# Linear attention and an ELU feed-forward on one core: the instruction orders of blocks three to six, solved anew

## The chip, the core and the metric

The kernel runs on one core of a Trainium2 chip. The metric is the device time of one execution in microseconds (us); the median of three runs of the kernel before is 292.15 us (291.99 to 292.51). The core has five engines with instruction streams of their own: TensorE (PE in the profile; its weight loads are listed apart as PEld), VectorE (DVE), ScalarE (ACT), GpSimd (POOL) and SyncE (SP), which here only issues transfers. Each engine executes its stream in order; an instruction that needs another engine's result waits at a semaphore, and everything behind it in the same stream waits with it.

## The reference

```python
# q, k, v: [8 batches, 8 heads, 576 positions, 64]
q_s = exp(q - max) / sum over the 64 features
k_s = exp(k - max) / sum over the 576 positions
kv  = einsum('bhsd,bhse->bhde', k_s, v)
attn = einsum('bhsd,bhde->bhse', q_s, kv)
x = attn.transpose(0, 2, 1, 3).reshape(4608, 512)
h = x @ w_in                                   # [4608, 2048]
g = where(h > 0, h, exp(min(h, 0)) - 1)        # ELU
out = g @ w_out                                # [4608, 512], float32
```

## The kernel before

**Attention.** Work goes by units, `n` = 0 to 15, each with half of a batch entry's eight heads. For a unit, k, v and q tiles are loaded (`load`, L361: 128 partitions by 1152 floats, 576 KB). ScalarE takes the exponential of k in place (L401) and of q (L397); VectorE sums q's exponentials over the features (L423) and inverts the sums (L425); POOL or VectorE scales q by them into `QS` (L435); v is converted to bfloat16 in `VB` by ScalarE or POOL (L279 with output VB). `QS` is transposed, from unit 4 on by a transposing transfer on the SP queue (L472) into `QT`, which ScalarE or POOL widens to `qsT` (L279). TensorE multiplies k and v (L509, 72 small matmuls a unit in the paired form), VectorE scales the result into the block-diagonal `MBLK` (L518, L522), and TensorE multiplies it with `qsT` (L540). The result is copied from PSUM into `XT`, the input of the feed-forward (L279 with output XT), by ScalarE or VectorE. There is one buffer for the v tiles of most units (`VR0`, called `vR0` in the planner), so the next v load cannot start before the conversion of the tile before has read it.

**Feed-forward.** Its rows go in nine blocks of 512 (`j` = 0 to 8). In each, eight groups (`g`) of two hidden tiles are computed on TensorE with eight 512-column matmuls (`hg_mm`, L622) into one of two pairs of PSUM banks. For each group ScalarE takes the exponential from PSUM into `GE` (L672) and then `relu(1 - exp)` in place (L674), and VectorE combines both with the PSUM value into `GR` in two halves (L678). Only then can TensorE overwrite that pair of banks with the next but one group.

**Output.** Blocks 0 and 1 are multiplied with `w_out` directly (L699, 512 columns). From block 2 on, pairs of rows are multiplied by a Strassen-like scheme with seven products in place of eight (`pair`, L832, 256 columns). It needs sums and differences of the `GR` tiles (`add_sum`, L783, by VectorE or POOL; some go to the tile `SB`) and, once, combinations of `w_out` (`combos`, L759, into `TB`). VectorE adds the products from PSUM into `OSB` (L841), PSUM copies to `OSB` are made by ScalarE or VectorE (L279), and SP stores `OSB` (L728).

**What sets the order.** Every instruction, or short run of matmuls, is an operation with a number, given in the order in which `program` creates it (0 to 1401). Its dependencies follow from the tiles that it reads and writes. The strings in `ORDER` list, for each engine, the numbers in the order in which it executes them. Where an operation may run on either of two engines, it runs on the one in whose list it stands:

```python
if alts:
    eng = self.home.get(len(self.ops))
    eng = eng if eng in alts else next(iter(alts))
    dur = alts[eng]
```

So a number that goes from the list "act" to the list "gp" moves that operation from ScalarE to POOL. Semaphore waits are placed from the dependencies. The lists are written out; nothing is reordered when the kernel is built, and the planner's own durations only decide how many spare matmuls fill TensorE's start.

Operations that the text below names:

| Numbers | What they are |
|---|---|
| 219 | k load; 234 is ScalarE's exponential of it |
| 362, 370 | VectorE's L678 of a group; TensorE's group that overwrites its banks |
| 396 | `w_out` combination into `TB`, 1024 columns, read by matmuls 506 |
| 403, 404 | narrower combinations, 512 columns |
| 451, 466, 467 and 474 | sums on `GR` tiles (256 columns; 474 has 512) |
| 473 | sum into `SB`, 512 columns; 461: L832 matmuls that 467 waits for |
| 601, 604, 767 | conversions of v tiles that share the buffer `VR0` |
| 602, 605 | the v loads into `VR0` after 601 and after 604 |
| 640, 643, 693, 695, 707, 779, 791 | sums on `GR` tiles; 779 is read by matmuls 787 |
| 666, 678, 699, 708, 729, 741 | groups of L622, eight matmuls each |
| 671, 672 | VectorE's L841 addition; the L832 matmuls that follow in its bank |
| 683 to 685 | L832 matmuls; sum 695 waits for 684 |
| 700 to 703 | L672, L674 and the two L678 of group 699, whose banks group 729 overwrites |

Of the kernel before, what the change touches and what calls it, by code (L numbers as in the profile page):

```python
# [50 lines left out]
    "act": (  # L51
# [12 lines left out]
    "dve": (  # L64
# [37 lines left out]
}  # L102

# [1013 lines left out]
```

## Time and profile before

| | |
|---|---|
| Time, median of 3 runs | 292.15 us |
| Time of the profiled execution | 292.0 us |
| Its span, first to last instruction | 290.2 us |
| Granted TensorE clock, mean | 0.999 |
| Busy: PE, PEld | 280.1, 243.7 us |
| Busy: DVE, ACT, POOL | 231.5, 212.1, 160.3 us |
| HBM read, written | 36.70 MB, 9.44 MB |

The profiled execution takes 1.8 us more than its span. The changed part of the orders begins at 62.1 us on SP, 67.4 us on VectorE, 69.2 us on TensorE, 71.4 us on POOL and 73.2 us on ScalarE, and ends at 203.6, 213.6, 214.0, 216.1 and 208.3 us.

A row of a view by groups gives line, engine, operation, output and input tiles, shape and count, then busy time in us and the mean of one in ns, then the idle time of the engine just before these instructions, with what ended it ("<-"). A row of the timeline gives start and length in us and merges neighbours of one kind. In the view of transfers, the time to landing runs from the issue to the arrival of the last byte. Busy times of matmuls overlap, since TensorE pipelines them and their ends are modelled.

### The profile page before, as it was taken

The page shows a single profiled execution, that of the slowest core. Times are in us where ns is not written, and L with a number is a line of the kernel's source. Part 1 is how long each engine was busy: PE and PEld are TensorE (multiplying, and loading weights), DVE is VectorE, ACT ScalarE, POOL GpSimd, SP SyncE. Part 2 cuts the span into 40 slices and gives each one's busy share as a digit, 9 for nine tenths or more (in the row PEclk, how much of TensorE's full clock was granted, in tenths as well). Part 3 has the DMA queues.
Part 4 walks back from the last instruction along what each step waited for, and adds up shares of the span by engine and source line. Part 5 has one row for each costly group of instructions (what it writes and reads, how often), then busy time and mean ns, then how long its engine had stood idle before and what let it go on. Part 6 is the DMA issues. An engine that isn't in the chain of part 4 may idle for free.

```text
span 290.2 us, 5483 instructions
## 1 busy us (share of the span) xinstructions
PE 280.1 (97%) x2176; PEld 243.7 (84%) x2176; DVE 231.5 (80%) x432; ACT 212.1 (73%) x237; POOL 160.3 (55%) x159
## 2 busy tenths in 40 slices
PE   2899999999999999999999999999999999999995
PEld 0488887888888899989899998989999999989995
DVE  3758847886699998898998879797785978668884
ACT  4858838989999877989887788857687546655510
POOL 1992443426356679409776793845417712794441
PEclk9999999999999999999999999999999999999999
DMA  7999999897989724775686457322211001400244
GB/s 260 395 369 388 390 388 357 219 212 253 267 246 292 209 103 111 248 189 172 133 267 198 122 82 277 69 48 52 63 36 38 0 2 30 114 0 20 56 97 123
DMA packets 36474, 50.04 MB, mean 172 GB/s; under 512 B 16352, under 2 KB 18144, under 8 KB 36448
## 3 DMA queue, kind: packets, MB, share of 16 engines
q1 hardware_dynamic: 29680, 33.96, 42.6%
q0 software_dynamic: 6528, 15.47, 17.6%
q8 instruction: 17, 0.28, 0.4%
q10 hardware_dynamic: 240, 0.26, 0.3%
q14 instruction: 9, 0.07, 0.1%
HBM read 36.70 MB, written 9.44 MB: 159 GB/s over the span
## 4 chain that ended last, share of the span: by engine, by line
PE 91%; DVE 3%; DMA 2%; POOL 2%; ACT 0%; SPq 0%; issue 0%
PE PS L622 44%; PE PS L832 32%; PE PS L699 9%; PE PS L540 3%; DMA KR<-in_k_dram 2%; PE PS L509 2%; DVE GR L678 1%; POOL W L379 1%; DVE QS L435 0%; DVE ZQ L423 0%; POOL VB L279 0%; PE PS L459 0%; POOL QS L435 0%; DVE MBLK L522 0%; ACT GE L674 0%; SPq L361 0%
## 5 line engine op out<-in xcount | busy, mean ns | idle before, releaser
L622 PE MATMUL PS<-XT,W 128*128 128x512 f32 x576 | 141.5, 393 | 0.1
L622 PEld LDWEIGHTS PS<-XT,W 128*128 128x128 f32 x576 | 105.3, 188 | 21.1 <-DVE GR L678 0.3
L678 DVE SCALAR_TENSOR_TENSOR GR<-PS,GE 128x512 fp32r<-128x512 f32 x112 | 76.7, 686 | 20.6 <-ACT GE L674 19.2
L672 ACT ACTIVATE GE<-PS 128x1024 f32<-128x1024 f32 x56 | 57.4, 1024 | 43.1 <-PE PS L622 36.2
L783 POOL TENSOR_TENSOR GR<-GR 128x256 fp32r<-128x256 f32 (+1 forms) x50 | 48.5, 981 | 47.7 <-DVE SB L783 29.0
L674 ACT ACTIVATE GE<-GE 128x1024 f32<-128x1024 f32 x56 | 59.4, 1060 | 1.5
L832 PE MATMUL PS<-TB,GR 128*128 128x256 f32 x336 | 52.5, 283 | 0.0
L832 PE MATMUL PS<-W,GR 128*128 128x256 f32 x336 | 52.2, 283 | 0.0
L832 PEld LDWEIGHTS PS<-TB,GR 128*128 128x128 f32 x336 | 46.5, 191 | 1.4 <-DVE OSB L841 0.3
L832 PEld LDWEIGHTS PS<-W,GR 128*128 128x128 f32 x336 | 46.5, 191 | 1.1
L435 POOL TENSOR_TENSOR QS<-QR,RZQ 128x1152 f16<-128x1152 f32 (+1 forms) x15 | 27.7, 1845 | 29.5 <-DVE RZQ L425 26.2
L841 DVE TENSOR_TENSOR OSB<-OSB,PS 128x256 f32<-128x256 f32 x84 | 34.8, 416 | 10.8 <-PE PS L832 9.3
L699 PE MATMUL PS<-W,GR 128*128 128x512 f32 x128 | 32.2, 394 | 0.0
L783 POOL TENSOR_TENSOR GR<-SB,GR 128x256 fp32r<-128x256 f32 (+1 forms) x26 | 25.4, 985 | 8.2 <-PE PS L832 7.4
L699 PEld LDWEIGHTS PS<-W,GR 128*128 128x128 f32 x128 | 23.6, 188 | 4.5
L423 DVE TENSOR_REDUCE ZQ<-QR 128x18 f32<-128x1152 f32 (+2 forms) x18 | 21.7, 1208 | 5.8 <-ACT QR L421 4.9
L783 POOL TENSOR_TENSOR SB<-GR 128x256 fp32r<-128x256 f32 (+1 forms) x19 | 18.6, 981 | 11.8 <-PE PS L832 7.1
L401 ACT ACTIVATE KR<-KR 128x1152 bf16<-128x1152 f32 x16 | 18.4, 1158 | 2.7 <-DMA KR<-in_k_dram 2.7
L783 DVE TENSOR_TENSOR GR<-GR 128x256 fp32r<-128x256 f32 (+1 forms) x34 | 19.9, 595 | 0.1
L397 ACT ACTIVATE QR<-QR 128x1152 f32<-128x1152 f32 x14 | 16.2, 1158 | 1.8 <-DMA QR<-in_q_dram 1.7
L279 POOL CAST VB<-VR 128x1152 bf16<-128x1152 f32 (+1 forms) x11 | 12.2, 1111 | 8.6 <-DMA VR<-in_v_dram 8.6
L832 PE MATMUL PS<-W,SB 128*128 128x256 f32 x104 | 16.8, 283 | 0.0
(67 smaller groups left out, 265.1 us busy)
## 6 DMA issues: line engine op xcount, KB each, us to landing
out_dram<-OSB SPq DMA_DIRECT2D x61, 128.0 KB, 2.4
QR<-in_q_dram SPq DMA_DIRECT2D x12, 576.0 KB, 5.4
KR<-in_k_dram SPq DMA_DIRECT2D x12, 576.0 KB, 5.4
VR<-in_v_dram SPq DMA_DIRECT2D x12, 576.0 KB, 5.7
W<-in_moe_w_out_dram POOLq DMA_DIRECT2D x4, 1024.0 KB, 16.3
QR<-in_q_dram POOLq DMA_DIRECT2D x4, 576.0 KB, 11.9
VR<-in_v_dram POOLq DMA_DIRECT2D x4, 576.0 KB, 13.0
KR<-in_k_dram POOLq DMA_DIRECT2D x4, 576.0 KB, 14.0
```

The costliest lines, as they stand in the source:

```text
L397: S.add("act", t_act(1152, False), lambda e: e.activation(flat(q), flat(q), AF.Exp), key - 3, X=[f"qR{i}0", f"qR{i}1"])
L401: S.add("act", t_act(1152, False), lambda e: e.activation(ek[:, :, :, :].rearrange("p h c d -> p (h c d)"), flat(k), AF.Exp), key - 2, X=[ ...
L423: S.add("dve", t_dve(m), lambda e, qp=qp, zp=zp: e.tensor_reduce(zp, qp, AX.X, ALU.add), key - 3, R=[f"qR{i}{x}" for x in xs], W=[f"ZQ{i}{ ...
L435: lambda e, qp=q[:, :, a:b, :], rz=rz, dst=qs[:, :, a:b, :]: e.tensor_tensor(dst, qp, rz, ALU.mult),
L622: last = e.matmul(P[:, t * 512:(t + 1) * 512], self.W1[:, kc, tt * 128:(tt + 1) * 128], self.XT[:, kc, rc:rc + BLK], start=(kc == 0), stop ...
L672: S.add("act", t_act(1024, True), lambda e: e.activation(ge, P, AF.Exp), key, W=own, X=banks)
L674: S.add("act", t_act(1024, False), lambda e: e.activation(ge, ge, AF.Relu, bias=1.0, scale=-1.0), key, X=own)
L678: S.add("dve", t_dve(512 if j else 1024), lambda e, u=u: e.scalar_tensor_tensor(*(x[:, :, u, :] if j else x for x in (gt, P)), 0.0, ge[:, ...
L699: last = e.matmul(dst, self.tile(jb, jj, ts), self.W2[:, jj, c0:c1], start=(jj == 0), stop=(jj == 15))
L783: lambda e: e.tensor_tensor(dst, a, b, op), key, R=R, W=W, X=X, after=after)
L832: last = e.matmul(dst, a[i][:, y_, :], b[i][:, y_, :], start=start and i == 0 and y_ == 0, stop=stop and i == len(grps) - 1 and y_ == z - ...
L841: S.add("dve", t_dve(256), lambda e: e.tensor_tensor(dst, a, b, ALU.add), key, R=R, W=W, X=X, after=after)
```

## The change

The lists of all five engines are replaced in the stretch from the third block to the sixth, about operations 288 to 1041. The operations, their numbers and their dependencies stay. 73 operations stand in another engine's list:

| From | To | Operations |
|---|---|---|
| DVE | POOL | 24: 14 sums of 256 and 5 of 512 columns, 4 `w_out` combinations, one scaling of q |
| POOL | DVE | 19: 11 sums of 256 and 8 of 512 columns |
| DVE | ACT | 14: 8 copies to `OSB`, 6 copies to `XT` |
| ACT | POOL | 8: 3 conversions of v, 5 widenings of `qsT` |
| ACT | DVE | 6: 5 copies to `XT`, one copy to `OSB` |
| POOL | ACT | 2 conversions of v |

ScalarE's list has 241 entries instead of 239, VectorE's 419 instead of 432, POOL's 166 instead of 155; TensorE's 457 and SP's 119 are in another order. The core of the diff (the rows that hold the places named above):

```diff
     "pe": (
-        "651 625 626 627 634 652 653 645 662 663 656 657 664 658 666 672 683 673 684 674 685 587 "
-        "678 687 688 589 689 714 690 691 715 692 716 699 598 708 725 719 726 720 721 727 606 729 "
-        "781 735 782 736 737 741 783 785 786 787 788 789 814 790 815 797 816 819 808 820 825 826 "
+        "625 651 626 652 653 627 634 645 656 657 658 662 663 664 683 684 685 666 672 673 674 587 "
+        "678 589 687 688 689 714 715 690 691 692 716 598 699 708 719 725 720 726 721 727 606 729 "
+        "735 781 782 736 737 741 783 785 786 787 788 797 789 790 814 815 816 808 825 819 820 826 "
...
     "act": (
-        "543 544 433 437 564 565 441 576 577 586 746 635 636 646 647 601 667 668 588 603 679 680 "
-        "600 597 700 713 701 709 757 710 730 731 752 742 743 767 798 799 809 769 810 830 831 909 "
+        "543 544 591 433 564 565 621 576 577 586 650 635 636 646 647 746 603 667 668 679 686 680 "
+        "600 604 700 701 709 710 607 757 730 731 784 742 743 909 813 798 799 809 810 830 831 770 "
...
     "gp": (
-        "163 132 164 201 206 204 209 228 231 307 238 397 401 325 393 417 406 398 462 473 450 435 "
-        "451 466 465 467 396 477 428 474 527 478 531 476 583 438 641 639 632 633 629 631 640 643 "
-        "594 644 693 695 749 694 696 604 706 705 707 791 779 793 780 795 792 796 805 760 802 803 "
+        "163 132 164 201 206 204 209 228 231 307 393 238 397 310 318 401 325 394 406 417 398 328 "
+        "400 473 451 403 466 404 467 474 396 477 435 428 529 531 532 528 530 431 438 539 583 630 "
+        "616 629 639 641 633 594 642 695 640 643 693 601 644 597 704 749 706 705 767 791 707 779 "
...
     "sp": (
-        "8 9 10 11 12 13 205 207 210 220 229 219 180 230 236 309 308 190 183 356 184 347 239 181 "
-        "249 357 189 319 187 248 326 186 348 320 418 392 377 391 329 378 338 419 494 495 511 510 "
-        "429 430 436 339 557 584 558 585 574 573 449 439 660 661 448 595 602 677 676 596 750 605 "
+        "8 9 10 11 12 13 205 207 210 220 229 187 189 183 181 219 180 190 230 184 236 309 308 357 "
+        "186 239 356 347 249 319 326 348 248 378 320 391 418 392 377 338 329 419 494 495 339 429 "
+        "510 511 436 430 558 557 584 585 573 574 439 448 449 595 661 660 602 677 676 596 605 751 "
```

81 rows, old and new, of the table ORDER are left out of this document.

## The prediction

> **What bounds the kernel now.** I read the page first (busy shares, then the chain of work that ended last), then busy time by stretch over the part whose orders change, then the waits of the weight loads, then single stretches of the timeline. The first two rows are of the page, the next four of the view by stretch (start and end, length, busy time and instructions of PE, PEld, DVE, ACT, POOL; granted clock, DMA share, GB/s), the last two all waits of the weight loads from 60 us to the end.
>
> ```profile
> PE 280.1 (97%) x2176; PEld 243.7 (84%) x2176; DVE 231.5 (80%) x432; ACT 212.1 (73%) x237; POOL 160.3 (55%) x159
> PE 91%; DVE 3%; DMA 2%; POOL 2%; ACT 0%; SPq 0%; issue 0%
> ...
> 67.00:100.00 33.00, 32.90 (x291) 27.46 (x290) 27.84 (x45) 31.38 (x35) 17.78 (x13) 1.00 0.85 248
> 100.00:140.00 40.00, 40.00 (x319) 36.07 (x318) 36.08 (x76) 34.64 (x38) 27.27 (x25) 1.00 0.55 159
> 140.00:180.00 40.00, 40.00 (x321) 36.12 (x320) 34.42 (x65) 32.89 (x35) 26.84 (x26) 1.00 0.72 194
> 180.00:216.00 36.00, 36.00 (x292) 32.48 (x291) 30.41 (x63) 25.56 (x30) 18.58 (x17) 1.00 0.24 56
> ...
> PEld PS L832 <- DVE OSB L841: 0.3, 1, 0.3
> PEld PS L622 <- DVE GR L678: 0.3, 1, 0.3
> ```
>
> TensorE is busy without a break at clock 1.00 all through the part that changes, and 91% of the chain is TensorE's. A busy TensorE need not be at its peak, so I count its work. The rows below: two pieces of the chain with nothing but one kind of matmul (start, length), the matmuls between 69.17 and 213.97 us (the first and the last place at which TensorE's order differs), and three neighbouring pieces of its timeline.
>
> ```profile
> 218.37 3.68 PE PS L622 x16
> 222.05 4.79 PE PS L832 x40
> ...
> L622 PE MATMUL PS<-XT,W 128*128 128x512 f32 x312 | 78.0, 394 | 0.1
> L832 PE MATMUL PS<-W,GR 128*128 128x256 f32 x192 | 30.6, 282 | 0.0
> L832 PE MATMUL PS<-TB,GR 128*128 128x256 f32 x184 | 29.1, 283 | 0.0
> L699 PE MATMUL PS<-W,GR 128*128 128x512 f32 x45 | 11.2, 390 | 0.0
> L832 PE MATMUL PS<-W,SB 128*128 128x256 f32 x64 | 10.1, 282 | 0.0
> ...
> 153.72 0.36 PE L540 MATMUL PS<-qsT,MBLK 128*128 128x192 f32 x2
> 154.02 0.78 PE L509 MATMUL PS<-VB,KR 64*64 64x65 bf16 x72
> 154.72 2.12 PE L622 MATMUL PS<-XT,W 128*128 128x512 f32 x8
> ```
>
> A 512-column matmul takes 3.68/16 = 0.23 us, a 256-column one 4.79/40 = 0.12 us. So 357 x 0.23 = 82.1 us and 440 x 0.12 = 52.8 us, together 134.9 of 144.8 us. A group of 72 small L509 matmuls takes 154.72 - 154.02 = 0.70 us, and there are five in the stretch (3.5 us); the 41 of L540 take about 0.15 us each by the pair at 153.72 (6.2 us). That makes 144.6 us. What can be won between the first and the last changed matmul is a few tenths: the two named waits, 0.6 us in all, and no more than about that again in what the rounding hides.
>
> **The change part by part.** Nothing is added or removed: the same 1402 operations with the same dependencies. Seventy-three change engine; the rest of the diff is order. TensorE's count of matmuls of each kind between its first and last difference is the same, so its own work is worth nothing either way, and only a wait can cost it time. The moves, each at the time of a row of the same shape:
>
> ```profile
> 140.57 0.74 POOL L783 TENSOR_TENSOR GR<-GR 128x256 fp32r<-128x256 f32 x1
> 157.40 1.30 POOL L783 TENSOR_TENSOR GR<-SB,GR 128x512 fp32r<-128x512 f32 x1 [1.70 <-PE PS L832]
> 151.91 1.15 POOL L279 CAST VB<-VR 128x1152 bf16<-128x1152 f32 x1
> 106.18 2.41 POOL L759 TENSOR_TENSOR TB<-W,TB 128x1024 fp32r<-128x1024 f32 x1
> 138.90 1.15 ACT L279 ACTIVATE VB<-VR 128x1152 bf16<-128x1152 f32 x1
> ```
>
> POOL receives 24 operations from VectorE (14 narrow sums at 0.74, five wide sums and three narrow combinations at 1.30, a wide combination at 2.41 and one 1152-column q scaling, taken at the same 2.41: 25.6 us) and eight 1152-column conversions from ScalarE (9.2 us); it gives 19 sums to VectorE (11 x 0.74 + 8 x 1.30 = 18.5 us) and two conversions to ScalarE (2.3 us). Net POOL works 14.0 us more in the stretch, ScalarE and VectorE less (14 PSUM copies also go from VectorE to ScalarE, six back). In the four rows above, POOL worked 90 of 149 us, so it has room on the average; VectorE, with 129 of 149 and 36.1 of 40 between 100 and 140 us, is relieved. On the average this speaks for the new orders, but TensorE did not wait for VectorE before, beyond the 0.6 us.
>
> The matmuls of operations 683, 684 and 685 (8 x 0.12 = 0.96 us) now stand ahead of group 666, so that operation 672, which waited 0.3 us for VectorE's L841 addition, comes later; I count -0.3 us. The other wait, before operation 370 at 86.6 us, keeps its neighbours and stays.
>
> Seven of the eight stores of the first block's output now stand earlier on SP, four of them ahead of k load 219:
>
> ```profile
> 62.08 1.31 SPq L361 DMA_DIRECT2D KR<-in_k_dram  x1
> 70.67 1.17 ACT L401 ACTIVATE KR<-KR 128x1152 bf16<-128x1152 f32 x1
> 72.15 1.03 ACT L672 ACTIVATE GE<-PS 128x1024 f32<-128x1024 f32 x1 [0.32 <-PE PS L622]
> ```
>
> At about 0.6 us of the queue each (two take 1.12 at 154.13, below) load 219 leaves at about 64.5 instead of 62.08 and lands 5.4 us later, at 69.9; ScalarE reads it at 70.67 and was then idle for 0.32 us. Cover of 0.8 us, so I count 0; with a landing of 6.5 us it would be 71.0, late by 0.3, which the idle time takes up. SP's other moves put a store (0.6 us) ahead of a load or behind one; 0 as well, and the three places below hold the loads for which that is not so.
>
> The tightest new place is at 138 to 154 us. Conversion 604 of a v tile moves from POOL to ScalarE, where it stands directly ahead of exponential 700; conversion 601, which frees the v buffer for the load 602 that 604 waits for, moves from ScalarE to POOL and stands behind four sums. So ScalarE now stops in the middle of its L672/L674 work until a load lands, and behind it wait 700, 701, then VectorE's 702 and 703, then TensorE's group 729, which overwrites their PSUM. The chain starts when matmuls 684 end:
>
> ```profile
> 149.84 1.03 ACT L672 ACTIVATE GE<-PS 128x1024 f32<-128x1024 f32 x1 [0.70 <-PE PS L622]
> 151.02 1.06 ACT L674 ACTIVATE GE<-GE 128x1024 f32<-128x1024 f32 x1
> 152.15 1.40 DVE L678 SCALAR_TENSOR_TENSOR GR<-PS,GE 128x512 fp32r<-128x512 f32 x2
> ...
> L361 SPq DMA_DIRECT2D VR<-in_v_dram x1: 580/580/580, 142.4 to 142.4; - x1
> DMA to landing us min/median/max: 6.4/6.4/6.4
> ...
> L361 SPq DMA_DIRECT2D VR<-in_v_dram x1: 383/383/383, 153.1 to 153.1; - x1
> DMA to landing us min/median/max: 4.0/4.0/4.0
> ...
> DMA to landing us min/median/max: 4.0/5.4/6.5
> ...
> 140.39 0.60 SPq L361 DMA_DIRECT2D KR<-in_k_dram  x1
> 141.03 1.32 SPq L472 DMA_TRANSPOSE QT<-QS  x1
> 154.13 1.12 SPq L728 DMA_DIRECT2D out_dram<-OSB  x2
> 155.29 0.59 SPq L361 DMA_DIRECT2D QR<-in_q_dram  x1
> ```
>
> POOL: sums 695, 640, 643, 693 and conversion 601, 0.74 + 1.30 + 0.74 + 1.30 + 1.15 = 5.2 us; then the load; then 604 (1.15), 700 (1.03), 701 (1.06), 702 and 703 (1.40): 4.6 us. With about 0.3 us of hand-overs that is 10.1 us and the load. TensorE's work from the end of 684 to 729 is 32 matmuls of 512 columns, 50 of 256, three pairs of L540 and one pair with 72 of L509: 7.4 + 6.0 + 0.9 + 1.0 = 15.3 us. The load may therefore take 5.2 us. The same load took 6.4 us before, right behind a k load and a transpose; all 27 loads on this queue from 60 to 180 us lie between 4.0 and 6.5. In the new order the k load and the transpose are long done, and two stores and a q load follow it: just the company of the load at 153.1 us, which took 4.0. So the stall is between 0 (1.2 us in hand) and 6.5 - 5.2 = 1.3 us; I take a load of 5.0 to 5.4 us, as it is nearer to the 4.0 row by its company but its followers come sooner, and count 0.2 us, the upper end.
>
> The second tight place follows from it: the next v load, 605, is issued when 604 has read the buffer; POOL's 767 (1.15) waits for it and behind it stand sums 791, 707 and 779 (1.30 + 0.74 + 0.74), the last of which matmuls 787 need. From 604's end that is the load and 4.1 us; TensorE has 3.6 us to 729 and 16 x 0.23 + 22 x 0.12 = 6.3 us from there to 787, so 5.8 us for the load. At the median of 5.4 it holds; I count 0.
>
> The third is POOL between 98 and 109 us: sum 473 and seven more operations up to combination 396 (three narrow sums at 0.74, two combinations and a wide sum at 1.30, then 2.41), 9.8 us in a row. Sum 467 waits for matmuls 461; from there POOL has 0.74 + 1.30 + 2.41 = 4.5 us, and TensorE 16 x 0.23 + 16 x 0.12 = 5.6 us until matmuls 506, which read 396. About 1 us in hand; I count 0.
>
> ```profile
> L783 DVE TENSOR_TENSOR SB<-GR x11: 413/682/1451, 90.9 to 192.2; 128x256 fp32r<-128x256 f32 x7, 128x512 fp32r<-128x512 f32 x4
> 149.34 2.63 POOL L783 TENSOR_TENSOR GR<-GR 128x512 fp32r<-128x512 f32 x2
> ```
>
> These rows show what can eat that: VectorE's wide sum takes 0.68 us alone and once 1.45 us, with POOL's two sums beside it at 2.63 instead of 1.30 + 0.74 = 2.04 us. The Trainium skill, page "SBUF — State Buffer", section "Who interferes with whom", has a rule for it: a VectorE instruction with two SBUF inputs and a GpSimd instruction that reads SBUF exclude each other, and the later one stands still until the other ends. The trace agrees with it here.
>
> Sum: 292.0 us (the profiled execution; its span is 290.2, with 1.8 us around it) - 0.3 + 0.2 = 291.9; the median of the runs, 292.15, lies 0.15 above the profiled one, so 292.1.
>
> **The rivals.** First, slower: ScalarE stands still for v load 602. If loads 602 and 605 take 6.4 us as the one at 142.4 us did, TensorE loses 6.4 - 5.2 = 1.2 us at 729 and 6.4 - 5.8 = 0.6 us at 787, 1.8 in all: 292.1 - 0.2 + 1.8 = 293.7. It decides from a load of 5.2 us. For it: the exponential at 149.84 us waited for TensorE, and now a DMA stands in the same line. Against: the company of the load. Second, also slower: POOL as the bound from 98 to 109 us. Each meeting of two-input operations can cost up to 1.45 - 0.68 = 0.77 us; five VectorE sums lie in that stretch, two full meetings (1.54) use up the 1 us in hand and 0.5 more: 292.6, and with the sums behind late too up to 293.2; I take 292.9. Against: three of the five come before sum 467's wait for 461, which evens them out. Third, faster: both named waits go and nothing is late: 292.15 - 0.6 = 291.5. Against: the neighbours of 370 stay. Fourth, that the orders leave no more slack than before: TensorE then stays the bound with about as many close hand-overs, and the time is the forecast's; this is part of it.
>
> **How the numbers follow.** Forecast (292.1, alone 291.6 to 292.7) 0.57; late v loads 0.27 (293.7); POOL 0.11 (292.9); faster 0.05. The range goes from 291.6, below which I leave 4 in 100, to 294.0, above which both stalls and followers of them would lie: it is the first rival's 293.7 and a little. A difference of 0.2% (0.58 us) is about what a measurement of this kernel can tell from none. Faster by more than that is only the third rival: 0.04. Slower are the first rival, half of the second, and a tail of the forecast: 0.37. The rest, 0.59, within.
>
> **What would show it.** Right: TensorE busy 40.00 of 40.00 in the stretches from 100 to 180 us again; the wait of L832's weight loads for L841 gone; POOL's busy time up by some 14 us, VectorE's down; a wait of ScalarE's VB conversion for the v load of about 1 to 2 us, without an entry for L622 behind VectorE's L678 near 153 us. Wrong: weight loads of L622 waiting for L678 there by 1 us, or of L832 for POOL's or VectorE's sums near 110 or 160 us; waits of over 0.6 us in sum anywhere; or a stretch of TensorE that is shorter than 144 us.

## The result and the profile after

The changed kernel takes 293.74 us (median of 4 runs, 293.53 to 294.5) against 292.22 us (291.99 to 292.51): 1.0051 times, 95% interval 1.0034 to 1.0068, so it is slower by about 1.5 us. The profiled execution took 293.63 us with a span of 291.8 us, against 292.0 and 290.2.

First the busy shares of the page of the changed kernel, then its view by stretch with the same bounds as before (start and end, length, busy time and instructions of PE, PEld, DVE, ACT and POOL; granted clock, DMA share, GB/s), then all waits of its weight loads from 60 us to the end. The line numbers of the changed file are one lower than those of before (L621 is L622 of before, and so on).

```profile
PE 280.5 (96%) x2176; PEld 243.3 (83%) x2176; DVE 228.2 (78%) x419; ACT 209.9 (72%) x239; POOL 175.0 (60%) x170
...
67.00:100.00 33.00, 32.29 (x289) 26.75 (x288) 24.79 (x40) 29.45 (x35) 23.07 (x16) 1.00 0.90 236
100.00:140.00 40.00, 40.00 (x321) 36.20 (x320) 35.58 (x73) 33.17 (x39) 32.87 (x28) 1.00 0.64 189
140.00:180.00 40.00, 40.00 (x318) 36.15 (x318) 35.26 (x66) 32.56 (x35) 29.68 (x28) 1.00 0.66 181
180.00:216.00 36.00, 35.02 (x289) 31.57 (x289) 28.19 (x55) 25.68 (x31) 17.03 (x16) 1.00 0.26 47
...
PEld PS L621 <- DVE GR L677: 1.2, 1, 1.2
PEld PS L539 <- POOL VB L278: 1.1, 1, 1.1
```

POOL works 14.7 us more. TensorE is still at full clock and without a break from 100 to 180 us. It has a hole in the first stretch (0.71 us) and in the last (0.98 us), and there are exactly two waits to go with them, one for POOL and one for VectorE. The two 0.3 us waits of before are both gone.

**The first hole: a v load that left late.** SP's timeline of the changed kernel (start, length, engine, line, operation), then POOL's and TensorE's around the wait, then from the view of transfers issued between 62 and 70 us the size and the time from issue to landing.

```profile
62.43 3.15 SPq L727 DMA_DIRECT2D out_dram<-OSBX  x4
65.62 0.59 SPq L360 DMA_DIRECT2D KR<-in_k_dram  x1
66.26 1.13 SPq L727 DMA_DIRECT2D out_dram<-OSBX  x2
67.43 0.59 SPq L360 DMA_DIRECT2D QR<-in_q_dram  x1
68.07 0.59 SPq L727 DMA_DIRECT2D out_dram<-OSBX  x1
68.70 0.58 SPq L360 DMA_DIRECT2D VR<-in_v_dram  x1
...
70.33 2.42 POOL L758 TENSOR_TENSOR TB<-W 128x1024 fp32r<-128x1024 f32 x1
75.34 1.15 POOL L278 CAST VB<-VR 128x1152 bf16<-128x1152 f32 x1 [2.60 <-DMA VR<-in_v_dram]
...
76.55 0.47 PE L539 MATMUL PS<-qsT,MBLK 128*128 128x192 f32 x2 [0.71 <-POOL VB L278]
...
VR<-in_v_dram SPq DMA_DIRECT2D x1, 576.0 KB, 6.6
```

The same load, conversion and matmuls before, with the one store that stood ahead of the load:

```profile
63.44 0.55 SPq L728 DMA_DIRECT2D out_dram<-OSBX  x1
...
65.39 0.37 SPq L361 DMA_DIRECT2D VR<-in_v_dram  x1
...
71.37 1.15 POOL L279 CAST VB<-VR 128x1152 bf16<-128x1152 f32 x1 [0.94 <-DMA VR<-in_v_dram]
...
75.59 0.36 PE L540 MATMUL PS<-qsT,MBLK 128*128 128x192 f32 x2
...
VR<-in_v_dram SPq DMA_DIRECT2D x1, 576.0 KB, 5.9
```

Seven stores now stand ahead of v load 236, where one did before. The first four hold SP for 3.15 us, 0.79 each. The load leaves 68.70 - 65.39 = 3.3 us later and takes 0.7 us longer, so POOL's conversion 238 starts 4.0 us later. POOL's combination at 70.33, which now stands ahead of 238, is not the cause: POOL was idle for 2.60 us behind it until the load landed. TensorE's stream stops ahead of operation 240, which begins with the L539 matmuls at 76.55 us.

**The second hole: a sum of 0.4 us that took 2.3.** The timeline of the changed kernel around TensorE's group 979, and below it the same sum (operation 954) before.

```profile
197.05 2.14 POOL L434 TENSOR_TENSOR QS<-QR,RZQ 128x1152 f16<-128x1152 f32 x1
197.15 2.32 DVE L782 TENSOR_TENSOR SB<-GR 128x256 fp32r<-128x256 f32 x1
199.50 1.42 DVE L677 SCALAR_TENSOR_TENSOR GR<-PS,GE 128x512 fp32r<-128x512 f32 x2
200.97 0.99 PEld L621 LDWEIGHTS PS<-XT,W 128*128 128x128 f32 x5 [1.18 <-DVE GR L677]
```

```profile
192.25 0.42 DVE L783 TENSOR_TENSOR SB<-GR 128x256 fp32r<-128x256 f32 x1
```

Sum 954 reads two SBUF tiles. It began 0.10 us behind POOL's scaling of q (operation 922) and ended 0.28 us behind its end (199.47 against 199.19). Combinations 950 and 951 stand behind 954 on VectorE, and TensorE's group 979 overwrites the banks that they read. Before, 954 ran some 5 us earlier, and POOL did its wide sum 952 ahead of 922.

**Where the time went, section by section.** TensorE's groups 273, 349, 409, 575, 729, 904 and 979 (eight matmuls of L621 or L622 each) come in this order in every kernel here. The times between their first matmuls, in us, cut the stretch into six sections. The start of group 273 itself, ahead of every edit, lies between 58.0 and 59.5 us from one profiled execution to the next, so a section compares kernels better than a profiled total does. The last column is the median of the timed runs.

| Kernel | 273 to 349 | to 409 | to 575 | to 729 | to 904 | to 979 | sum | median |
|---|---|---|---|---|---|---|---|---|
| before | 18.52 | 22.00 | 29.35 | 26.79 | 33.72 | 10.93 | 141.30 | 292.22 |
| changed | 19.50 | 21.69 | 29.36 | 26.62 | 33.58 | 12.07 | 142.82 | 293.74 |
| e1 | 18.57 | 21.66 | 29.41 | 26.62 | 33.58 | 12.05 | 141.89 | 292.90 |
| e2 | 19.46 | 21.66 | 29.36 | 26.62 | 33.58 | 10.93 | 141.61 | 292.36 |
| e3 | 18.55 | 21.66 | 29.36 | 26.62 | 33.58 | 10.93 | 140.71 | 291.39 |
| e4 | 19.50 | 22.76 | 29.38 | 26.81 | 33.72 | 10.92 | 143.09 | 293.25 |
| f1 | 19.18 | 21.68 | 29.36 | 26.62 | 33.58 | 11.25 | 141.66 | 292.43 |
| f2 | 18.55 | 21.66 | 29.36 | 26.62 | 33.56 | 10.93 | 140.69 | 291.35 |
| f3 | 18.54 | 21.66 | 29.38 | 27.66 | 33.73 | 10.93 | 141.90 | 292.94 |
| g4 | 18.52 | 21.65 | 29.35 | 27.11 | 33.73 | 10.93 | 141.28 | 292.18 |
| g5 | 18.57 | 21.67 | 29.33 | 28.03 | 33.58 | 10.93 | 142.10 | 292.74 |
| g6 | 18.55 | 21.66 | 29.36 | 26.62 | 33.58 | 12.06 | 141.83 | 292.68 |

The changed kernel loses 0.98 us in the section with the late v load and 1.14 in the one with the long sum. It gains 0.31 + 0.17 + 0.14 = 0.62 in three others. That makes about +1.5 in the sections (the remaining one moves by 0.01), and the medians differ by 1.52. The new orders are better than the old ones in three of six sections; two places spoil them.

### The profile page after: what moved, and what is told of

It reads as the page before. It is cut to its first block, busy times and chain, and to the rows that moved or that the text cites. A ratio compares the mean times of both kernels' runs of the same rounds, so it can differ in the third digit from the quotient of the medians.

```text
span 291.8 us, 5469 instructions
## 1 busy us (share of the span) xinstructions
PE 280.5 (96%) x2176; PEld 243.3 (83%) x2176; DVE 228.2 (78%) x419; ACT 209.9 (72%) x239; POOL 175.0 (60%) x170
## 4 chain that ended last, share of the span: by engine, by line
PE 82%; DMA 9%; POOL 4%; DVE 3%; ACT 1%; issue 0%; SPq 0%
PE PS L621 38%; PE PS L831 30%; PE PS L698 8%; DMA W<-in_moe_w_out_dram 5%; PE PS L539 2%; DMA VR<-in_v_dram 2%; DMA KR<-in_k_dram 2%; POOL W L378 2%; PE PS L508 2%; DVE GR L677 1%; POOL VB L278 1%; DVE SB L782 1%; DVE OSB L840 0%; PE PS L458 0%; POOL QS L434 0%; ACT GE L673 0%
## 5 line engine op out<-in xcount | busy, mean ns | idle before, releaser
L621 PE MATMUL PS<-XT,W 128*128 128x512 f32 x576 | 141.4, 393 | 1.0 <-DVE GR L677 1.0
L621 PEld LDWEIGHTS PS<-XT,W 128*128 128x128 f32 x576 | 105.4, 188 | 22.2 <-DVE GR L677 1.2
L782 POOL TENSOR_TENSOR GR<-GR 128x256 fp32r<-128x256 f32 (+1 forms) x47 | 45.1, 969 | 35.9 <-DVE SB L782 25.3
L673 ACT ACTIVATE GE<-GE 128x1024 f32<-128x1024 f32 x56 | 59.5, 1063 | 1.5
L434 POOL TENSOR_TENSOR QS<-QR,RZQ 128x1152 f16<-128x1152 f32 (+1 forms) x16 | 30.4, 1902 | 21.6 <-DVE RZQ L424 19.5
L782 POOL TENSOR_TENSOR GR<-SB,GR 128x256 fp32r<-128x256 f32 (+1 forms) x26 | 24.5, 948 | 18.1 <-DVE GR L782 9.8
L782 POOL TENSOR_TENSOR SB<-GR 128x256 fp32r<-128x256 f32 (+1 forms) x22 | 21.4, 977 | 7.6 <-DVE GR L677 6.5
L782 DVE TENSOR_TENSOR GR<-GR 128x256 fp32r<-128x256 f32 (+1 forms) x37 | 21.3, 587 | 0.1
L278 ACT ACTIVATE OSB<-PS 128x256 f32<-128x256 f32 (+1 forms) x24 | 9.7, 408 | 14.7 <-PE PS L831 14.2
L278 ACT ACTIVATE XT<-PS 128x640 fp32r<-128x640 f32 (+6 forms) x22 | 12.8, 585 | 6.2 <-PE PS L539 3.0
```

The costliest lines, as they stand in the source:

```text
L278: return e.activation(dst, src, AF.Copy) if e is self.nc.scalar else e.tensor_copy(dst, src)
L434: lambda e, qp=q[:, :, a:b, :], rz=rz, dst=qs[:, :, a:b, :]: e.tensor_tensor(dst, qp, rz, ALU.mult),
L621: last = e.matmul(P[:, t * 512:(t + 1) * 512], self.W1[:, kc, tt * 128:(tt + 1) * 128], self.XT[:, kc, rc:rc + BLK], start=(kc == 0), stop ...
L673: S.add("act", t_act(1024, False), lambda e: e.activation(ge, ge, AF.Relu, bias=1.0, scale=-1.0), key, X=own)
L782: lambda e: e.tensor_tensor(dst, a, b, op), key, R=R, W=W, X=X, after=after)
```

## The experiments

Each kernel was timed beside the kernel before, whose median was 292.15 to 292.19 us in the three groups of runs (e; f; g). The theory: late load and long sum are independent, each costs about 1 us, and together they are the whole loss.

**e1: SP's loads ahead of its stores.** The changed kernel with one edit of SP's order, which puts loads 219, 230 and 236 back to where they stood before (store 180 is between them, as it was):

```diff
-"229 187 189 183 181 219 180 190 230 184 236 309"
+"229 219 180 230 236 187 189 183 181 190 184 309"
```

> The changed kernel, but on SP the loads 219, 230 and 236 stand ahead of the seven stores of the first block's output, as they did before. Theory: TensorE's wait before operation 240 at 76.6 us (0.9 us in the changed kernel) comes from v load 236, which left at 68.7 instead of 65.4 us; it goes, 236 leaves at 65.4 to 66.0 us, the time falls by about 0.9 us to 292.8, and the wait before group 979 stays at 1.2 us. Rival (the wide combination 393, which stands ahead of conversion 238 on POOL, or the stores' traffic itself): 238 still starts after 74 us, the wait stays above 0.5 us and the time at 293.3 or more.

292.90 us, 1.0026 times before (1.0017 to 1.0035). The wait at 240 is gone, the one at 979 stays. The section is back at 18.57.

**e2: sum 954 moved earlier on VectorE.** The changed kernel with:

```diff
-"920 921 896 907 908 967 968 775 776 777 778 954 950 951"
+"920 921 896 954 907 908 967 968 775 776 777 778 950 951"
```

> The changed kernel, but VectorE's sum 954 (256 columns) stands behind 896, as before, instead of between 778 and 950. Theory: the 1.2 us wait of group 979 comes from 954 standing still for 1.9 us while POOL's q scaling 922 (2.1 us) runs; it goes, 954 takes at most 1.2 us beside a short POOL sum, and the time falls by about 1.2 us to 292.5; the wait before 240 stays. Rival (979 waits because VectorE is behind in general there, with 967, 968 and the four operations 775 to 778 ahead of 950): 950 and 951 move up only by 0.4 us and 0.8 us of the wait stays, 293.3.

292.36 us, 1.0006 times (0.9982 to 1.003); its runs spread from 291.33 to 295.63, so the interval is wide. Four of the twelve took 291.33 to 291.48 us, as short as e3 below, though the profiled execution (292.44 us) has the first hole in full. So the late load seems not to cost its time in every execution; no trace shows one in which it does not. In VectorE's timeline of e2 the sum is short again, and the last section is 10.93:

```profile
192.96 0.42 DVE L782 TENSOR_TENSOR SB<-GR 128x256 fp32r<-128x256 f32 x1
```

**e3: both edits.**

> The changed kernel with both edits. Theory: the two waits are the whole loss; 291.7 to 292.2, level with the kernel before or up to 0.3 us below it, since the kernel before's waits at 86.6 and 140.5 us (0.3 us each) are gone in the changed one. Rival (the 73 moves to other engines, 14 us more on POOL, cost something besides): 292.6 or more, with waits elsewhere.

291.39 us, 0.9977 times before (0.9968 to 0.9986). This beats both kernels, and lies a little below what was expected. No wait of TensorE or its weight loads is left in the stretch, and in the view by stretch of e3 both holes are closed:

```profile
67.00:100.00 33.00, 33.00 (x293) 27.64 (x292) 25.72 (x40) 30.29 (x36) 23.88 (x16) 1.00 0.88 244
...
180.00:216.00 36.00, 36.00 (x293) 32.51 (x293) 27.39 (x58) 26.74 (x32) 16.97 (x16) 1.00 0.25 54
```

**e4: the stores alone, in the kernel before.** The kernel before, with the six stores moved ahead of v load 236 that the changed kernel moves there:

```diff
-"229 219 180 230 236 309 308 190 183 356 184 347 239 181 249 357 189 319 187 248"
+"229 187 189 183 181 219 180 190 230 184 236 309 308 356 347 239 249 357 319 248"
```

> The kernel before with only one part of the change: the seven stores on SP stand ahead of the loads as in the changed kernel. Theory: v load 236 leaves about 3 us later, conversion 238 ends near 76.5 us and TensorE waits about 0.9 us before operation 240: 293.1. Rival (the stores matter only together with the moves on POOL and ScalarE): 292.2, no wait there.

293.25 us, 1.0035 times (1.0013 to 1.0056), again with widely spread runs (291.77 to 295.2). The same section loses the same 0.98 us as in the changed kernel. In the profiled execution, the slowest of the ten, 0.76 more is lost in the next section, where a v load is late too. There VectorE's and POOL's timelines show the second mechanism, in both directions:

```profile
82.60 1.15 POOL L279 CAST VB<-VR 128x1152 bf16<-128x1152 f32 x1 [2.14 <-DMA VR<-in_v_dram]
83.70 3.51 POOL L759 TENSOR_TENSOR TB<-W 128x1024 fp32r<-128x1024 f32 x1
...
82.75 2.21 DVE L435 TENSOR_TENSOR QS<-QR,RZQ 128x1152 f16<-128x1152 f32 x1
```

VectorE's q scaling 318 began 0.15 us behind POOL's conversion and took 2.21 us. In the timeline of before it took 1.36:

```profile
80.48 1.36 DVE L435 TENSOR_TENSOR QS<-QR,RZQ 128x1152 f16<-128x1152 f32 x1
```

POOL's 1024-column combination in e4 began while 318 was still running, and took 3.51 us in place of 2.42.

**f1: POOL's q scaling behind its wide sum.** Two explanations of the second hole were left: what POOL does at that moment, or simply the place of 954 directly ahead of 950 and 951. f1 is the changed kernel with VectorE's order untouched and one number moved on POOL:

```diff
-"957 944 922 952 1008"
+"957 944 952 922 1008"
```

> The changed kernel with its q scaling 922 on POOL moved behind sum 952; VectorE's order, with sum 954 behind 778, as in the changed kernel. Theory (the two engines exclude each other, and the later one stands still): 954 now meets POOL's wide sum 952 (1.3 us) or nothing, takes 0.4 to 1.5 us instead of 2.32, and group 979 waits 0 to 0.4 us instead of 1.24: 292.5 to 292.9. Rival (the place of 954 in VectorE's list, ahead of combinations 950 and 951, is what costs, whatever POOL does): 979 waits 1.2 us as before, 293.7.

292.43 us, 1.0004 times (0.9994 to 1.0014). POOL's and VectorE's timelines of f1:

```profile
196.86 1.32 POOL L782 TENSOR_TENSOR SB<-GR 128x512 fp32r<-128x512 f32 x1
196.96 1.50 DVE L782 TENSOR_TENSOR SB<-GR 128x256 fp32r<-128x256 f32 x1
198.12 2.32 POOL L434 TENSOR_TENSOR QS<-QR,RZQ 128x1152 f16<-128x1152 f32 x1
```

The sum again starts 0.10 us behind a POOL instruction and ends 0.28 us behind its end, only this one takes 1.32 us in place of 2.14. So POOL's instruction sets the sum's length; the place in VectorE's list only decides whether TensorE has to wait for it. The last section is 11.25, 0.32 longer than without the meeting and 0.82 shorter than with the longer one. The rest of f1's gain over the sections is not of this edit: its first hole came out 0.32 us shorter (19.18 against 19.50).

The Trainium skill, page "SBUF — State Buffer", section "Who interferes with whom", has it as "Issue order, not op shape, decides who blocks": the later of a VectorE instruction with two SBUF inputs and a GpSimd instruction that reads SBUF stands still until the other ends. Here the trace agrees four times: 2.32 and 1.50 us for a 0.42 us sum, 2.21 for a 1.36 us scaling, and 3.51 for POOL's 2.42 us combination. It agrees to within 0.2 us: the later instruction always ended 0.14 to 0.17 us sooner than the other's end plus its own time alone. The trace of before has a fifth case, POOL's q scaling beside a sum of VectorE's that takes 0.42 us alone:

```profile
147.25 2.12 POOL L435 TENSOR_TENSOR QS<-QR,RZQ 128x1152 f16<-128x1152 f32 x1 [3.29 <-DMA QT<-QS]
...
148.72 0.94 DVE L783 TENSOR_TENSOR GR<-GR 128x256 fp32r<-128x256 f32 x1
```

The scaling had 0.65 us left when the sum began, and the sum took 0.52 us longer.

**f2 and g5: the price of the first rival.** In the changed kernel the place at 138 to 154 us did not stall. Timelines of ScalarE, VectorE and TensorE there (conversion 604, combinations 702 and 703, group 729):

```profile
149.53 1.17 ACT L278 ACTIVATE VB<-VR 128x1152 bf16<-128x1152 f32 x1 [0.74 <-DMA VR<-in_v_dram]
...
152.95 1.42 DVE L677 SCALAR_TENSOR_TENSOR GR<-PS,GE 128x512 fp32r<-128x512 f32 x2 [0.49 <-ACT GE L673]
...
155.32 1.45 PE L621 MATMUL PS<-XT,W 128*128 128x512 f32 x5
```

152.95 + 1.42 = 154.37, which leaves 0.95 us to 155.32. f2 is e3 with v load 602 behind two stores and a q load on SP; g5 is f2 with POOL's conversion 601, which frees the buffer of 602, behind two more operations:

```diff
-"595 661 660 602 677 676 596 605 751"
+"595 661 660 677 676 596 602 605 751"
```

```diff
-"643 693 601 644 597 704"
+"643 693 644 597 601 704"
```

> The changed kernel with both repairs (SP's loads ahead of its stores, sum 954 earlier; 291.4 us) and v load 602 moved three places down on SP, behind two stores and a q load, 1.6 to 1.8 us later. If the place at 138 to 154 us is as tight as the first rival of the prediction had it, with 0.95 us in hand before 729 in the profile of the changed kernel: TensorE waits 0.6 to 0.9 us before 729, and up to 0.5 us more before 787: 292.0 to 292.8. If there is room beyond the 0.95 us: no wait, 291.4.

> f2 (291.35 us) with POOL's conversion 601 moved behind 644 and 597, 1.9 us later, so that v load 602 leaves 1.9 us later again. In f2's profile VectorE's combination 703 ended 0.05 us before group 729 started, so the hand is used up. If the mechanism of the prediction's first rival is right: TensorE waits 1.4 to 1.9 us before 729 and no more than that in sum, 292.7 to 293.3. If the conversion or the exponentials have room elsewhere: no wait, 291.4.

f2 took 291.35 us, 0.9967 times before (0.9955 to 0.9979), no slower than e3: the guess of 0.6 to 0.9 us was wrong. SP issued the transfers moved ahead while the load was still waiting for 601, so it left 0.05 us behind them and 0.2 us behind 601's end; it only landed later, 5.1 us after its issue in place of 4.1. The same three engines in f2:

```profile
149.79 1.17 ACT L278 ACTIVATE VB<-VR 128x1152 bf16<-128x1152 f32 x1 [1.86 <-DMA VR<-in_v_dram]
...
152.99 1.42 DVE L677 SCALAR_TENSOR_TENSOR GR<-PS,GE 128x512 fp32r<-128x512 f32 x2 [1.40 <-ACT GE L673]
...
154.46 2.11 PE L621 MATMUL PS<-XT,W 128*128 128x512 f32 x8
```

VectorE now ends at 154.41, 0.05 us ahead of TensorE: the time in hand is used up to the last tenth, and nothing was lost. In g5 the load leaves at 147.07 us in place of 144.67, but lands in 3.9 us, so that 604 starts 1.15 us later, 1.4 later counted from group 273:

```profile
150.94 1.17 ACT L278 ACTIVATE VB<-VR 128x1152 bf16<-128x1152 f32 x1 [3.27 <-DMA VR<-in_v_dram]
...
154.14 1.42 DVE L677 SCALAR_TENSOR_TENSOR GR<-PS,GE 128x512 fp32r<-128x512 f32 x2 [2.06 <-ACT GE L673]
...
155.61 1.21 PE L621 MATMUL PS<-XT,W 128*128 128x512 f32 x4 [1.12 <-DVE GR L677]
```

g5 took 292.74 us, 1.0019 times before (1.0008 to 1.0029), that is 1.39 more than f2, and its section to 729 is 28.03 in place of 26.62. From the edge on, lateness of that load is paid in full. The rival's mechanism is right; the changed kernel stays 0.95 us short of it.

**f3 and g4: where the gain comes from.** e3 is 0.59 us shorter than before in the sections. f3 puts two pieces of the change into the kernel before: matmuls 683 to 685 ahead of group 666, and q scaling 318 on POOL in place of VectorE.

```diff
 pe
-"658 666 672 683 673 684 674 685 587"
+"658 683 684 685 666 672 673 674 587"
 dve
-"244 318 245"
+"244 245"
 gp
-"401 325"
+"401 318 325"
```

> The kernel before with only TensorE's matmuls 683, 684 and 685 moved ahead of group 666 and q scaling 318 moved from VectorE to POOL, ahead of 325. Theory (what the repaired kernel gains over the one before is the two waits of TensorE, before 370 and before 672, 0.4 to 0.6 us in all): both waits gone, 291.6 to 291.8. Rival (the gain is elsewhere, in steps that the waits do not show): 292.1 to 292.2.

292.94 us, 1.0026 times (1.0015 to 1.0037): slower, against the expectation. The section to 409 gains what was expected (21.66 in place of 22.00), but the one to 729 loses 0.87. The waits of the weight loads in f3, then VectorE and TensorE at the place:

```profile
PEld PS L832 <- DVE OSB L841: 0.7, 1, 0.7
PEld PS L540 <- ACT qsT L279: 0.4, 1, 0.4
...
139.58 0.88 DVE L841 TENSOR_TENSOR OSB<-OSB,PS 128x256 f32<-128x256 f32 x2 [0.42 <-PE PS L832]
...
140.05 1.22 PE L832 MATMUL PS<-W,GR 128*128 128x256 f32 x8 [0.51 <-DVE OSB L841]
```

Matmuls 683 write the bank that VectorE's addition 659 reads, and 659 waits for matmuls 658, which in f3 stand directly ahead of 683. The changed kernel moves 656, 657 and 658 as well, ahead of 662 to 664, which gives VectorE the time. g4 is f3 with that:

```diff
-"662 663 656 657 664 658 666 672 683 673 684 674 685 587"
+"656 657 658 662 663 664 683 684 685 666 672 673 674 587"
```

> The kernel before with q scaling 318 on POOL, as in f3, and with TensorE's matmuls 656 to 685 in the order of the changed kernel: 656, 657 and 658 ahead of 662, 663 and 664, then 683, 684, 685, then group 666. Theory (683 waits for VectorE's addition 659, which waits for 658; with 658 some 0.7 us earlier nothing is late): the waits at 370, 672 and 683 are all gone, 0.5 us less than before in TensorE's stretch: 291.6 to 291.8. Rival (683 to 685 ahead of 666 cost by themselves): 683 waits 0.5 us or more again, 292.5 or more.

292.18 us, 1.0001 times (0.9992 to 1.001). The wait for 659 shrinks to 0.2 us, but the one of matmuls 598 for ScalarE's widening to `qsT`, 0.4 us in f3 and g4 and not there before, stays, and the section to 729 is 27.11 against 26.79 before. So neither outcome held: the 0.17 us that the changed kernel gains there do not come from TensorE's moves alone. In g4 that widening (operation 597) stands on ScalarE and ends at 150.08 us, 0.05 ahead of matmuls 598. In the changed kernel it is one of the five widenings moved to POOL and ends at 147.14, 1.25 ahead of 598, which does not wait; no run makes this move by itself. The gain of 0.34 us in the section to 409 is reproduced by itself; the other 0.3 us belong to the whole order and were not taken apart further.

**g6: which load it was.** e1 moved three loads. g6 is the changed kernel with v load 236 alone moved, ahead of three stores and a q load; the k load 219 stays late.

```diff
-"181 219 180 190 230 184 236 309"
+"181 219 236 180 190 230 184 309"
```

> The changed kernel with one edit on SP: v load 236 moved ahead of store 180, directly behind k load 219; the four stores stay ahead of both, so the k load leaves as late as in the changed kernel. If the late v load alone makes the wait before operation 240: wait gone, 292.8 to 293.0, as in e1. If the late k load counts too: part of the 0.9 us stays, 293.2 or more.

292.68 us, 1.002 times before (1.0011 to 1.0029). Load 219 leaves at 64.72 us, 2.6 us later than before (65.62 in the changed kernel), and yet k's exponential 234 starts at 70.81, against 70.67 before. The section is 18.55, as in e1 and e3, and of the weight loads' waits in g6 only this one is left:

```profile
PEld PS L621 <- DVE GR L677: 1.2, 1, 1.2
```

The late v load alone is the first hole; the k load costs nothing.

## Why the prediction was wrong, point by point

- **TensorE is the bound, and at most a few tenths can be won.** Right. e3, where no wait is left, is 0.59 us shorter than before over the sections and 0.8 us in the medians, against "0.6 us in all, and no more than about that again".
- **POOL works 14.0 us more.** Right: 14.7. The q scaling that moved (318) took 2.12 us on POOL, not the 2.41 that was taken for it.
- **The wait at 672 goes, -0.3.** The wait went, and its section gained 0.17. The reason given was only half of it: f3 shows that 683 to 685 wait 0.7 us there unless 658 moves too, which the prediction did not mention.
- **The wait before 370 stays.** Wrong, to the good. Its neighbours stay, but q scaling 318, 1.36 us of VectorE's work at 80.5 us, left VectorE's queue ahead of them; f3 and g4 show this move, with no other change in that section, taking the wait away.
- **The seven stores on SP count 0.** Wrong: this is the first failed step. It followed the stores to k load 219, the first load behind them, and settled the rest with "SP's other moves put a store (0.6 us) ahead of a load or behind one; 0 as well". V load 236, the third load behind the burst, stands behind all seven stores. Before, its conversion ended at 71.37 + 1.15 = 72.52 us and matmuls 240 started at 75.59, so there were 3.1 us in hand. For 219 the count of 0 was right (g6). The size was off as well: in the burst of four the stores took 0.79 us each, not 0.6. The term should have been 3.3 us of the queue and 0.7 of slower landing, less the 3.1 in hand: 0.9. The section lost 0.98.
- **The place at 138 to 154 us, +0.2.** The bound on the load (5.2 us) was good: the changed kernel's load took 4.1 and left 0.95 in hand, f2's took 5.1 and left 0.05. The argument from the load's company was right too. So the 0.2 should have been 0, and the first rival, whose 293.7 lies next to the measured time, did not happen: the same total came from two other places. That the measured time lies beside the rival's, and inside a range whose upper end was set by that rival, is luck.
- **The meetings of VectorE and POOL.** The mechanism was named and right; place and price were not. It was looked for only between 98 and 109 us, where TensorE stayed busy, and priced at 0.77 us a meeting, from one row with POOL's sums. A meeting costs nearly what is left of the other's instruction: at 197 us that was a q scaling of 2.14 us, so 1.9. The sum at 148.72 us in the trace of before, held up by such a scaling, was not looked at. This is the second failed step; the edit that made it (922 ahead of 952 on POOL, 954 behind 778 on VectorE) was not priced at all, and its section lost 1.14.

In the forecast's own sum: for the -0.3 and the +0.2 the sections show -0.62 in all and no stall, and two terms that stood at nothing were 0.98 and 1.14. That makes +1.5 us in place of -0.1.

## What to carry to other kernels

When orders move transfers on a queue, follow every load behind the moved stores to the first instruction that needs it, and charge it with the sum of the issue times ahead; the first load behind them may have cover that the third has not. When work goes from VectorE to GpSimd, list where a two-input VectorE operation now stands beside a long GpSimd instruction, and keep short sums that sit ahead of the critical combination away from it. A schedule that gains in most places and loses in two is repaired by moving a few numbers: with two short edits the changed kernel went from 1.5 us behind to 0.8 us ahead.

## What the runs showed of the hardware

- A VectorE sum of 0.42 us took 2.32 us behind POOL's 2.14 us instruction, and 1.50 behind one of 1.32 us: it ended 0.28 us behind the other both times. One with 0.65 us of a POOL instruction left before it took 0.94. POOL's 2.42 us combination took 3.51 when VectorE had begun first.
- Four stores of 128 KB in a row held SP for 3.15 us (3.31 in e4, 2.86 in g6), a pair at 66.26 us 1.13.
- The 576 KB loads on SP between 60 and 215 us landed 4.0 to 7.3 us after their issue in the changed kernel and 3.7 to 8.1 over all runs. V load 602 took 4.1, 5.1 and 3.9 us in the changed kernel, f2 and g5, with other transfers issued around it.
- Sections of TensorE's stream without a wait and in the same order repeat to within 0.1 us across kernels (29.33 to 29.41 from group 409 to 575), while the start of the stretch moves by 1.5 us between executions.
